# Attention and two feed-forward layers on one core: the last block's tokens staged in another tile ring, and three edits beside it

## The chip, the cores and the metric

The kernel runs on one core of one Trainium2 chip. The metric is the device time of one execution in microseconds (us); lower is better.

## The reference

```python
scores = scale * np.matmul(q, k.transpose(0, 1, 3, 2))       # 4 batches, 8 heads, 576 x 576, head size 64
scores = np.where(block_i >= block_j, scores, -1e9)           # blocks of 64 positions
attn   = softmax(scores);  x = attn @ v                       # -> 2304 tokens x 512
h = x @ w_in;   x = (h * sigmoid(h)) @ w_out                  # layer 1, 512 -> 2048 -> 512
h = x @ w_in2;  x = (max(h,0) + alpha * min(h,0)) @ w_out2    # layer 2, same sizes
```

All tensors are float32. The kernel keeps float32 accuracy by splitting each operand into a high part that TensorE can multiply and a low part that holds the rest; each product is then three matmuls (high x high, high x low, low x high; `three`, L1027).

## The kernel before, in words

**Tokens.** The 2304 tokens form nine blocks of 256 (T1, T2). Blocks 0 to 3 are positions 0 to 255 of the four batches, blocks 4 to 7 positions 256 to 511, and block 8 the last 64 positions of all four batches together.

**Stages.** Attention runs per batch and pair of heads as 32 jobs (L1017). Their outputs are the tokens of layer 1, kept in `x_all` in two places: blocks of even number in one, of odd number in the other (L517). Block 8 is written to DRAM instead (`x_last`, L992, 16 stores from all the late jobs) and read back by `load_last` (L525) as two tiles `xl` of 128x512 float32 once place 0 of `x_all` is free of block 6. Layer 1 runs in 72 steps `d` (L1380), mixed with the attention that feeds later blocks. Steps 0 to 15 are blocks 0 and 1, then each block has eight steps: block 6 has 48 to 55. Steps 56 to 58 are block 7 alone, 59 to 68 blocks 7 and 8 together, 69 to 71 block 8 alone. A step has three parts: `up1` (L1035, matmuls into PSUM tile `h`, two places), `act1` (L1068) and, one step later, `down1` (L1081). `store1` (L1103) turns a finished block with VectorE into tiles `x2e` and stores them to DRAM. Layer 2 then reads the blocks back (`load2`, L1127, tiles `xs`).

**`act1`** computes h * sigmoid(h): ScalarE writes tanh(h/2) to tile `t`, VectorE forms (t+1)*h in `t` (L1075), ScalarE copies the high part to `g`, and `split` (L329, low part at L335) computes the low part of `g` on GpSimd for blocks 2 to 6 and on VectorE for the others (L1077).

**Rings.** A tile tag has a fixed number of places, taken in the order of creation: tile number i waits until tile i minus the count is done with. Tag `t` (ff1 pool) has two, shared by the `t` tiles of `act1`, the `x2e` tiles of blocks up to 6, and the two `xl` tiles. Around step 56 the order of that ring is: `t` of step 56, two `x2e` of block 6, two `xl`, `t` of step 57, `t` of step 58. Tag `p` (att pool) has three places of the same 2 KB per partition, used for attention probabilities. The att pool is closed, and its memory reused by the pool ff2, when the first ff2 tile is made (L293).

**Weights of layer 2** are read twice. A first reading takes the largest absolute value (`scan_w`, L457: tiles `scani` in the two places of att tag `st`, `scano` in four of ff2 tag `scan`; the maximum at L469 on VectorE). `scale_w` (L489) turns it into a scale: `spread` (L444) carries a per-partition maximum to all partitions with one ScalarE copy into `ar` (the tag `ar2`), one 128-column matmul (L449) and one VectorE maximum (L451). `load2` for the first two blocks of layer 2 uses `spread` too (L1140). A second reading (`raw1i`, `raw1o`) splits the weights (L350, L386).

**Order.** Nothing is scheduled at run time: the kernel collects operations with an engine, a cost and a due time `at`, and `Plan.order` (L150) simulates the engines and writes out the order; of the operations ready at an engine's next free moment it takes the one with the lowest `at`. Each engine runs its own list strictly in order, waiting on semaphores. All DMAs but eight run through SyncE's list (SP), so a DMA whose data is late holds back those behind it. In the model a DMA costs 0.5 us of SP and `extra` of the shared queue (KiB / 350):

```python
dma_free = max(dma_free, start + min(o.cost, 0.63) + 0.65) + o.extra   # L200
o.end = dma_free + 0.95                                                # L201
```

Of the kernel before, what the change touches and what calls it, by code (L numbers as in the profile page):

```python
# [8 lines left out]
F32 = mybir.dt.float32  # L9
# [4 lines left out]
AF = mybir.ActivationFunctionType  # L14
# [15 lines left out]
T1 = 256  # L30
# [29 lines left out]
SLOTS = ((256, 256, 4), (384, 576, 10))  # L60

LEAD = 2.0
LOAD, PREPARE, PREPARE_V = -6.4, -2.5, -0.11
SCORES, WEIGHTS, NEXT, LAST, OUTPUT = 0.0, 0.4, 0.44, 1.03, 1.47

# [42 lines left out]
class Plan:  # L108
# [41 lines left out]
    def order(self):  # L150
        engines = {}
        for o in self.ops:
            engines.setdefault(o.engine, 0.0)
        ready = {e: [] for e in engines}
        blocked = {}
        heads = {tag: 0 for tag in self.rings}
        dma_free = 0.0

        def offer(o):

            new = {}
            for b in o.bufs:
                if not b.started:
                    old = b.order[b.index - b.bufs] if b.index >= b.bufs else None
                    if heads[b.tag] + new.get(b.tag, 0) != b.index or (old is not None and old.free_at is None):
                        blocked.setdefault(b.tag, []).append(o)
                        return
                    new[b.tag] = new.get(b.tag, 0) + 1
                    if old is not None:
                        o.ready = max(o.ready, old.free_at + 0.2)  # L170
            ready[o.engine].append(o)

        for o in self.ops:
            if not o.waits:
                offer(o)
        done = []
        while len(done) < len(self.ops):
            best = None
            for e, lst in ready.items():
                if not lst:  # L180
                    continue
                free = engines[e]
                start = max(free, min(o.ready for o in lst))
                if best is None or start < best[0]:
                    best = (start, e)
            assert best is not None, "the order of the tiles' places leaves nothing that can start"
            start, e = best
            o = min((o for o in ready[e] if o.ready <= start), key=lambda o: (o.at, o.index))

            fresh = [b for b in o.bufs if not b.started]  # L190
            lost = [b for b in fresh if b.index - heads[b.tag] != sum(c.tag == b.tag and c.index < b.index for c in fresh)]
            ready[e].remove(o)
            if lost:
                blocked.setdefault(lost[0].tag, []).append(o)
                continue
            o.start = start
            engines[e] = start + o.cost
            o.end = start + o.cost
            if e == "DMA":
                dma_free = max(dma_free, start + min(o.cost, 0.63) + 0.65) + o.extra  # L200
                o.end = dma_free + 0.95  # L201
            done.append(o)
            recheck = []
            for b in o.bufs:
                if not b.started:
                    b.started = True
                    heads[b.tag] += 1
                    recheck.append(b.tag)
                b.left -= 1
                if b.left == 0:  # L210
                    b.free_at = max(p.end for p, _, _ in b.accesses)
                    recheck.append(b.tag)
            for p in o.after:
                p.waits -= 1
                p.ready = max(p.ready, o.end + self.HOPS[e].get(p.engine, 0.0) + (p.slack if p.engine != e else 0.0))
                if not p.waits:
                    offer(p)
            for tag in recheck:
                for p in blocked.pop(tag, []):
                    offer(p)  # L220
        self.span = max(o.end for o in done)
        return sorted(done, key=lambda o: (o.start, o.index))
# [27 lines left out]
def block_causal_attention_silu_prelu(  # L250
# [16 lines left out]
    B, PAIRS = qkv_b.shape[:2]  # L267
    FIRST = 2
# [10 lines left out]
    plan = Plan()  # L279
# [8 lines left out]
    ff_p = ctx.enter_context(tc.tile_pool(name="ff1", bufs=1))  # L288
# [24 lines left out]
    def sb(pool, shape, dtype, tag, bufs=1, name=None):  # L313
        return Buf(plan, pool, shape, dtype, tag, bufs, name)
# [129 lines left out]
    def spread(src, reads, dst, writes, tag="o"):  # L444

        t = ps(tag)
        ar = sb(ff2_p, [128, 1], F32R, "ar2", 2)
        act(1, lambda: ar(), src, AF.Copy, reads, [ar])
        add("PE", 0.12, lambda: nc.tensor.matmul(  # L449
            t()[:, 0:128], ar().to_broadcast([128, 128]), eye_r(), start=True, stop=True), [ar, eye_r], [t])  # L450
        add("DVE", dve_cost(128), lambda: nc.vector.tensor_reduce(dst(), t()[:, 0:128], axis=AX.X, op=ALU.max), [t], writes)  # L451
# [73 lines left out]
    def load_last():  # L525
        x = x_parts(2 * B)
        for kk in range(0, KD, 2):
            t = sb(ff_p, [128, 2, T1], F32, "t", 2, name="xl")
            dma(lambda t=t: t(),
                lambda kk=kk: x_last()[kk * 128:(kk + 2) * 128].rearrange("(k p) t -> p k t", p=128), 256,  # L530
                [x_last], [t])
            split(2 * T1, lambda kk=kk: x()[:, 0, kk:kk + 2], lambda kk=kk: x()[:, 1, kk:kk + 2], lambda t=t: t(),
                  [t], [(x, (0, kk))], [(x, (1, kk))], "DVE")
# [534 lines left out]
    def act1(step):  # L1068

        h = hs.pop(step)  # L1070
        t = sb(ff_p, [128, 2, T1], F32, "t", 2)
        g = sb(ff_p, [128, 2, 2, T1], F32R, "g", 2)
        h3 = lambda: h().rearrange("p (c t) -> p c t", c=2)
        act(2 * T1, lambda: t(), h3, AF.Tanh, [h], [t], psum=True, scale=0.5)
        add("DVE", dve_cost(2 * T1), lambda: nc.vector.scalar_tensor_tensor(  # L1075
            t(), t(), 1.0, h3(), op0=ALU.add, op1=ALU.mult), [t, h], [t])
        split(2 * T1, lambda: g()[:, 0], lambda: g()[:, 1], lambda: t(), [t], [(g, 0)], [(g, 1)],  # L1077
              "POOL" if FIRST <= step[1][0] < 2 * B - 1 else "DVE")
        gs[step] = g

    def down1(step):  # L1081
# [298 lines left out]
    for d in range(-20, total + 1):  # L1380
        attend(d + 1.0)

        plan.at = float(d - AHEAD)
        for at in range(d + AHEAD):
            for w in need.get(at, []):
                if w in first:
                    first.remove(w)
                    load_w(0, *w)
        plan.at = d - 0.5
        for kind, m in need.get(d + 1, []):  # L1390
            split_w(0, kind, m, aside=d + 1 <= ASIDE and m % 2 == 1)
        if d < 0:
            continue
        plan.at = float(d)
        if d < total:
            up1(seq[d])
            plan.at = d + 0.3
            act1(seq[d])
        if d >= 1:
            plan.at = d + 0.5  # L1400
            down1(seq[d - 1])
            for n, m in sorted(set(seq[d - 1])):
                if m == edge[n][1]:
                    plan.at = d + 0.6
                    store1(n)
        if d == LAST_AT:
            assert not pieces
            load_last()

        if d == LAST_AT:  # L1410
            ends += [o for b in plan.rings["x_last"] for o, _, _ in b.accesses]
            for m in range(MF):
                plan.at = SCAN[2] + SCAN[3] * m
                scan_w("o", m, ends)
            scanned = scans[:]
        if d == SCAN_AT:
            for j, m in enumerate(order2[NOT_AHEAD:]):
                plan.at = SCAN[0] + SCAN[1] * j
                scan_w("i", m, ())
        if d == last_up[order2[0]] + 1:  # L1420
            for m in order2[:NOT_AHEAD]:
                plan.at = last_up[m] + 1.7
                load_w(1, "i", m)
                greatest("i", m, staged[1, "i", m])
            plan.at = last_up[order2[0]] + 1.0
            scale_w("i", ends)
            plan.at = SCAN[2] + SCAN[3] * MF
            scale_w("o", ends)
        for m in order2:
            if last_up[m] == d - 1:  # L1430
                plan.at = d + 0.7
                if m not in order2[:NOT_AHEAD]:
                    load_w(1, "i", m)
                split_w(1, "i", m)
        if d == (NB - 1) * ND + 2:
            load2(0, after=ends)
            plan.at += 2.0
            load2(1)
# [137 lines left out]
```

## Time and profile before

| | |
|---|---|
| three runs | 897.29, 898.02, 899.15 us (median 898.02) |
| the profiled execution | 898.74 us, of which the profiled span is 897.0 us and 1.7 us lie around it |
| busy share of the span | PE 98%, PE weight loads 84%, VectorE (DVE) 79%, ScalarE (ACT) 52%, GpSimd (POOL) 31% |
| DMA | 130 GB/s mean over the span |
| TensorE clock | 0.999 of full speed, 2.4 GHz |

In the profile's rows times are in us from the start of the span. A row of the timeline has start, duration, engine, line, operation, output <- inputs and, in square brackets, how long the engine sat idle before it and which event ended that wait. Neighbouring instructions of one kind are merged into one row (xN). PEld is the weight load of TensorE, which overlaps its matmuls (PE); SPq is SyncE issuing DMAs.

### The profile page before, as it was taken

To read this page: it belongs to the slowest core of one execution; us is meant where nothing else is said; L and a number is where in the kernel's file an instruction comes from. 1 tells how busy PE (TensorE), PEld (TensorE's weight loads), DVE (VectorE), ACT (ScalarE), POOL (GpSimd) and SP (SyncE) were. 2 spreads that over 40 slices of the span, in tenths; PEclk is the share of its full clock that TensorE was granted. 3 is DMA by queue.
4 is the path that set the end of the run, shared out by engine and by line. 5 is a ranking of instruction groups with operands and counts; after the bars stand their busy time and mean duration, and the time that the engine had idled before them with its cause. 6 is when DMAs were issued, how large, how long until landed. Compare 5 with 4: busy or idle time off the path is not lost.

```text
span 897.0 us, 18472 instructions
## 1 busy us (share of the span) xinstructions
PE 879.4 (98%) x6941; PEld 749.4 (84%) x6941; DVE 706.7 (79%) x1572; ACT 464.0 (52%) x1061; POOL 281.9 (31%) x412
## 2 busy tenths in 40 slices
PE   7899999999999999999999999999999999999997
PEld 5688888898898989888878887666888888888886
DVE  5999767688898888898458899898887867677574
ACT  6987556677777877776224774333322222222211
POOL 6601002232222312222100000357645445454552
PEclk9999999999999999999999999999999999999999
DMA  8962133567566675669788893242101110000010
GB/s 299 408 246 53 36 78 94 146 130 158 112 153 145 114 175 116 128 153 189 218 279 338 288 343 126 97 164 77 46 28 27 49 28 27 25 28 25 1 24 24
DMA packets 134249, 116.56 MB, mean 130 GB/s; under 512 B 100240, under 2 KB 111504, under 8 KB 134160
## 3 DMA queue, kind: packets, MB, share of 16 engines
q1 hardware_dynamic: 133008, 111.19, 44.8%
q0 software_dynamic: 1152, 4.19, 1.2%
q8 instruction: 54, 0.88, 0.5%
q14 instruction: 35, 0.29, 0.1%
HBM read 78.65 MB, written 14.16 MB: 103 GB/s over the span
## 4 chain that ended last, share of the span: by engine, by line
PE 62%; DMA 3%; DVE 2%; ACT 1%; issue 1%; POOL 0%; DVEq 0%; SPq 0%; ACTq 0%
PE h L1030 20%; PE acc L1030 18%; PE e L1030 12%; PE s L1030 5%; PE o L1030 3%; DMA scani<-w_in 2%; PE e L734 2%; PE o L908 1%; DMA raw1i<-w_in 1%; PE s L734 1%; PE o L918 0%; ACT p L325 0%; DVE stat L852 0%; DMA xl<-x_last 0%; DVE t L1075 0%
## 5 line engine op out<-in xcount | busy, mean ns | idle before, releaser
L1030 PE MATMUL h<-x_all,w0i 128*128 128x256 f32 (+1 forms) x1464 | 223.6, 304 | 2.2 <-DVE t L1075 1.3
L1030 PEld LDWEIGHTS h<-x_all,w0i 128*128 128x128 f32 x1464 | 200.2, 190 | 21.1 <-issue 3.8
L1030 PEld LDWEIGHTS <-w1i 128*128 128x128 f16 x1728 | 168.9, 98 | 23.3 <-issue 0.5
L1211 POOL TENSOR_TENSOR u<-u 128x128 f32<-128x128 f32 x224 | 136.0, 627 | 125.6 <-DVE u L1203 105.7
L325 ACT ACTIVATE g<-u 128x896 f16<-128x896 f32 (+1 forms) x72 | 63.2, 878 | 215.1 <-POOL u L1211 138.8
L1030 PE MATMUL acc<-w0o,g 128*128 128x512 f32 x672 | 168.5, 394 | 0.6 <-POOL g L335 0.6
L1030 PEld LDWEIGHTS <-g 128*128 128x128 f16 x1368 | 133.9, 98 | 32.7
L1030 PEld LDWEIGHTS acc<-w0o,g 128*128 128x128 f32 x672 | 122.5, 188 | 27.4 <-issue 2.5
L335 POOL TENSOR_TENSOR g<-t,g 128x512 fp32r<-128x512 f32 x40 | 53.0, 1326 | 162.2 <-ACT g L325 158.2
L1030 PE MATMUL acc<-xh,w1i 128*128 128x256 f16 x864 | 100.2, 273 | 0.0
L1030 PE MATMUL h<-xh,w1i 128*128 128x256 f16 x864 | 99.2, 273 | 0.0
L1224 DVE SCALAR_TENSOR_TENSOR g<-u,g 128x896 f16<-128x896 f32 (+1 forms) x72 | 76.4, 1062 | 10.6 <-ACT g L325 10.6
L325 ACT ACTIVATE p<-p,stat 128x512 f16<-128x512 f32 (+2 forms) x112 | 63.3, 608 | 23.0 <-ACT p4b L325 7.0
L1199 DVE TENSOR_SCALAR u<-acc,alpha_sb 128x256 f32<-128x256 f32 x72 | 32.2, 478 | 46.3 <-PE acc L1030 45.0
L325 ACT ACTIVATE p<-e,stat 128x256 f32<-128x256 f32 (+2 forms) x98 | 50.9, 526 | 33.4 <-DVE stat L946 22.3
L325 ACT ACTIVATE t<-h 128x512 f32<-128x512 f32 x72 | 42.9, 596 | 42.7 <-PE h L1030 37.1
L1030 PE MATMUL e<-w1om,g 128*128 128x256 f16 x504 | 64.2, 273 | 0.0
L1075 DVE SCALAR_TENSOR_TENSOR t<-t,h 128x512 f32<-128x512 f32 x72 | 49.0, 680 | 9.2 <-ACT t L325 8.1
L325 ACT ACTIVATE g<-t 128x512 fp32r<-128x512 f32 x72 | 45.3, 629 | 18.1 <-DVE t L1075 17.5
L885 DVE SCALAR_TENSOR_TENSOR p<-p,stat,p 128x384 f16<-128x384 f32 (+1 forms) x64 | 48.4, 796 | 4.3 <-ACT p L325 4.1
L1030 PE MATMUL e<-w1op,g 128*128 128x256 f16 (+1 forms) x264 | 49.5, 311 | 0.0
L1030 PE MATMUL e<-w0o,g 128*128 128x512 f32 x192 | 49.0, 393 | 0.0
(167 smaller groups left out, 1328.0 us busy)
## 6 DMA issues: line engine op xcount, KB each, us to landing
st<-qkv_b SPq DMA_DIRECT2D x16, 800.0 KB, 4.9
raw0i<-w_in SPq DMA_DIRECT2D x16, 512.0 KB, 9.9
raw0o<-w_out SPq DMA_DIRECT2D x16, 512.0 KB, 10.0
scano<-w_out SPq DMA_DIRECT2D x16, 512.0 KB, 6.5
raw1i<-w_in SPq DMA_DIRECT2D x16, 512.0 KB, 5.6
raw1o<-w_out SPq DMA_DIRECT2D x16, 512.0 KB, 5.2
scani<-w_in SPq DMA_DIRECT2D x13, 512.0 KB, 4.4
x<-x2e SPq DMA_DIRECT2D x18, 256.0 KB, 2.5
```

Of the source, the lines that this page charges most:

```text
L325: nc.scalar.activation(dst(), src(), func, **k)
L335: eng.tensor_tensor(lo(), src(), hi().bitcast(F32), op=ALU.subtract)
L734: yield lambda n=n, a=a, b=b: nc.tensor.matmul(dst, w[rows, a, q0:q0 + m], w[rows, b, nq + k0:nq + k1], start=(n == 0), stop=(n == 2))
L885: add("DVE", dve_cost(n, 1, 1), lambda hl=hl, rr=rr, pr=pr: nc.vector.scalar_tensor_tensor(hl()[:, :, 1], pr(), rr(), hl()[:, :, 0], op0=A ...
L908: nc.tensor.matmul(o()[64 * r:64 * r + 64, q0:T1], self.v(r, kt, cv), self.turned(r, kt, cp, q0), start=(kt == 0 and n == 0), stop=(kt == ...
L1030: nc.tensor.matmul(dst, lhs(a), rhs(b), start=(start and n == 0), stop=(stop and n == 2))
L1075: add("DVE", dve_cost(2 * T1), lambda: nc.vector.scalar_tensor_tensor(t(), t(), 1.0, h3(), op0=ALU.add, op1=ALU.mult), [t, h], [t])
L1199: add("DVE", dve2_cost(T2, 1), lambda c=c, m=m: nc.vector.tensor_scalar(u()[:, 2 * c:2 * c + 2].rearrange("p i t -> p (i t)"), h()[:, T2 * ...
L1211: add("POOL", pool2_cost(128, 2.5), lambda out_=out_, x=x, y=y, op=op: nc.gpsimd.tensor_tensor(u()[:, out_], u()[:, x], u()[:, y], op=op), ...
L1224: add("DVE", dve2_cost(blocks * 128, 0, True), lambda: nc.vector.scalar_tensor_tensor(side(1)(), src(), 2.0**-G_EXP, side(0)(), op0=ALU.mu ...
```

## The change

- `load_last` takes its two `xl` tiles from tag `p` of the att pool (three places) instead of tag `t`, its due time moves from d + 0.6 (that of block 6's stores) to d + 0.2, and the modelled size of each load from 256 to 700 KiB.
- In `act1` the low parts of block 6 are computed on VectorE instead of GpSimd.
- In `spread` the ScalarE copy counts in the model as done 1.5 us later, so the matmul after it is placed later in TensorE's list.
- In `Plan.order` a DMA is not started before the eighth last has landed.

```diff
+LATE = 1.5
+LANES = 8
@@ order
+        landed = []
...
                 free = engines[e]
+                if e == "DMA" and len(landed) >= LANES:
+                    free = max(free, landed[-LANES])
                 start = max(free, min(o.ready for o in lst))
...
             engines[e] = start + o.cost
-            o.end = start + o.cost
+            o.end = start + o.cost + (o.extra if e == "ACT" else 0.0)
             if e == "DMA":
                 dma_free = max(dma_free, start + min(o.cost, 0.63) + 0.65) + o.extra
                 o.end = dma_free + 0.95
+                landed.append(o.end)
@@ spread
-        act(1, lambda: ar(), src, AF.Copy, reads, [ar])
+        act(1, lambda: ar(), src, AF.Copy, reads, [ar]).extra = LATE
@@ load_last
-            t = sb(ff_p, [128, 2, T1], F32, "t", 2, name="xl")
+            t = sb(att_p, [128, 2, T1], F32, "p", 3, name="xl")
             dma(lambda t=t: t(),
-                lambda kk=kk: x_last()[kk * 128:(kk + 2) * 128].rearrange("(k p) t -> p k t", p=128), 256,
+                lambda kk=kk: x_last()[kk * 128:(kk + 2) * 128].rearrange("(k p) t -> p k t", p=128), 700,
@@ act1
-              "POOL" if FIRST <= step[1][0] < 2 * B - 1 else "DVE")
+              "POOL" if FIRST <= step[1][0] < 2 * B - 2 else "DVE")
@@ the main loop
         if d == LAST_AT:
             assert not pieces
+            plan.at = d + 0.2
             load_last()
```

## Rows read from the trace of the kernel before

**Rows 1.** The page, first part: busy time, share of the span, instructions.
```profile
PE 879.4 (98%) x6941; PEld 749.4 (84%) x6941; DVE 706.7 (79%) x1572; ACT 464.0 (52%) x1061; POOL 281.9 (31%) x412
```

**Rows 2.** Waits of PE from 380 to 545 us: total, times, longest.
```profile
PE h L1030 <- DVE t L1075: 1.3, 1, 1.3
PE o L449 <- ACT ar L325: 1.1, 1, 1.1
PE acc L1030 <- POOL g L335: 0.6, 1, 0.6
PE h L1030 <- DVE x_all L998: 0.2, 1, 0.2
```

**Rows 3.** Timeline from 446 to 455 us: block 6's stores, then `xl`.
```profile
446.24 1.91 SPq L317 DMA_DIRECT2D x<-x2e  x2
...
448.32 1.97 SPq L317 DMA_DIRECT2D xl<-x_last  x2
...
450.30 3.03 PE L1030 MATMUL h<-x_all,w0i 128*128 128x256 f32 x24
450.40 1.83 SPq L317 DMA_DIRECT2D scano<-w_out  x4
...
453.17 0.58 ACT L325 ACTIVATE t<-h 128x512 f32<-128x512 f32 x1
...
453.91 0.68 DVE L1075 SCALAR_TENSOR_TENSOR t<-t,h 128x512 f32<-128x512 f32 x1
...
454.64 2.35 PE L1030 MATMUL h<-x_all,w0i 128*128 128x512 f32 x9 [1.31 <-DVE t L1075]
```

**Rows 4.** Tile `x_last`, 420 to 460 us: two of its stores, both `xl` loads.
```profile
L317 SPq DMA_DIRECT2D x_last<-xf x2: 326/671/1016, 423.5 to 438.1; - x2
...
DMA to landing us min/median/max: 2.7/3.4/5.2
```

**Rows 5.** Timeline from 432 to 441 us: low part of step 54, block 7's tokens.
```profile
432.53 0.69 DVE L469 TENSOR_REDUCE wmaxi<-scani 128x1 f32<-128x512 f32 x1 [0.36 <-DMA scani<-w_in]
432.91 1.29 POOL L335 TENSOR_TENSOR g<-t,g 128x512 fp32r<-128x512 f32 x1 [9.80 <-ACT g L325]
...
434.25 0.50 PE L1030 MATMUL acc<-w0o,g 128*128 128x512 f32 x1 [0.55 <-POOL g L335]
...
439.62 0.48 DVE L998 SCALAR_TENSOR_TENSOR x_all<-o,sc,x_all 128x256 fp32r<-128x256 f32 x1
```

**Rows 6.** Chain that ended last, from 420 to 445 us.
```profile
434.55 4.45 DMA scani<-w_in
...
440.15 1.94 PE h L1030 x14
```

**Rows 7.** Timeline: L746 alone, and beside a low part on GpSimd.
```profile
377.99 0.87 DVE L746 SCALAR_TENSOR_TENSOR v<-st,sc,v 128x640 f16<-128x640 f32 x1
...
406.33 1.29 POOL L335 TENSOR_TENSOR g<-t,g 128x512 fp32r<-128x512 f32 x1
406.40 1.90 DVE L746 SCALAR_TENSOR_TENSOR v<-st,sc,v 128x640 f16<-128x640 f32 x1 [0.89 <-POOL v L743]
```

**Rows 8.** Windows of block 6: busy of PE, PEld, DVE, ACT, POOL; clock, DMA.
```profile
378.00:397.00 19.00, 19.00 (x173) 17.14 (x173) 16.68 (x43) 13.56 (x39) 3.59 (x4) 1.00 0.80 178
397.00:433.70 36.70, 36.70 (x319) 32.48 (x315) 28.02 (x73) 22.15 (x57) 6.92 (x7) 1.00 0.86 196
```

**Rows 9.** Timeline from 518 to 531 us: the product that waits, a later low part.
```profile
518.83 1.21 DVE L1136 TENSOR_REDUCE xsc<-xs 128x1 f32<-128x1024 f32 x1
...
520.43 0.33 PE L449 MATMUL o<-eye_r,ar 128*128 128x128 f32 x1 [1.07 <-ACT ar L325]
...
526.98 0.68 DVE L335 TENSOR_TENSOR g<-t,g 128x512 fp32r<-128x512 f32 x1
...
528.05 2.91 PE L1030 MATMUL acc<-w0o,g 128*128 128x512 f32 x12
```

**Rows 10.** Waits of SP from 0 to 60 us: total, times, longest.
```profile
SPq L317 <- DMA raw0i<-w_in: 11.5, 12, 1.4
```

## The prediction

> **What bounds the kernel now.** I read the page first. TensorE (PE) is busy for 879.4 of 897.0 us [rows 1], so a change pays only where it takes a gap out of PE's row or shortens PE's work; it does not touch PE's work. Next I asked PE's waits in the stretch the change reaches, 380 to 545 us. They are four single events, 1.31, 1.07, 0.55 and 0.21 us, 3.14 us together [rows 2]. Then the timeline around each: the 1.31 at 454.64 [rows 3], the 0.55 and 0.21 at 434.25 and 440.15 [rows 5, 6], the 1.07 at 520.43 [rows 9]. No more than 3.14 us, 0.35%, can be had there. The profiled execution took 898.74 us, 0.72 above the median of 898.02; the sum is made against 898.74, and the same gain is then taken from the median. The measurement can tell about 0.2%, 1.8 us, from no change.
>
> **The last block's tokens (`xl`).** PE waits 1.31 us at step 59 because its `h` place is free only after step 57's L1075, at 453.91 + 0.68 = 454.59. That instruction waits for tanh at 453.17, which waits for a place in ring `t`: the two `xl` tiles stand before it there, and they wait for block 6's `x2e` stores, so their loads go out only at 448.32 [rows 3]. Step 57's matmuls were over before those of step 58 began at 450.30, so tanh lost some 3 us.
> In ring `p` the load waits for the last `x_last` store only. That store goes out at 438.1; landings of this tile took 2.7 to 5.2 us [rows 4], so it is in DRAM by 443.3 at the latest. Two issues of some 0.4 us put SP at 444.1, ahead of the `x2e` stores due at 446.24, so the queue it is moved past is not held. With 2.7 us to land, the tokens are there by about 447, and their splits, each a ScalarE copy and a VectorE subtraction (0.68 us, as the low part in [rows 9]), end near 449. Step 57's tanh now needs the first `x2e` store landed: 446.24 + 2.7 = 448.9, then 0.58 and 0.68 give 450.2. PE asks for that place at 450.30 + 3.03 = 453.33, 3 us later. So the 1.31 us go; bounds 0 and 1.31, and I take 1.31 because of the 3 us to spare. What comes behind on SP is `scano`, at 450.40 now; its memory may lie over that of `p`, so it may have to wait for the splits near 449, which is still no later than now.
>
> **The product of a maximum.** Five products are made; only that of 520.43 holds PE, for 1.07 us: its input is copied after the maximum L1136, which ends at 518.83 + 1.21 = 520.04 [rows 9]. Put 1.5 us later in PE's list, it has about 12 matmuls of step 70 before it (3.03 / 24 = 0.126 us each [rows 3]), which need nothing from it. So PE arrives after 520.43. Its result is needed only by block 1's second-layer tokens, several us on. But PE is then 1.07 us earlier against VectorE, which the change does not speed up there. Next late is the low part that ends at 526.98 + 0.68 = 527.66; the third matmul of the group at 528.05 uses it, at 528.05 + 2 x 0.24 = 528.53, so 0.87 us are to spare [rows 9], and 0.20 of the 1.07 come back as a wait. I take 0.87; bounds 0 (if VectorE is late by more) and 1.07.
>
> **Block 6's low parts.** Eight leave GpSimd, 1.29 us each [rows 5], and come to VectorE at 0.68 us [rows 9]: 5.4 us more work there in about 60 us. For step 54 it decides a wait: GpSimd starts at 432.91 and PE waits until 434.25, 0.55 us. VectorE is in a scan maximum until 432.53 + 0.69 = 433.22, so the low part can end at 433.90 and PE waits some 0.25 instead [rows 5]. That 0.3 us does not reach the end: at 440.15 PE waits for L998, which stands in VectorE's list behind a scan maximum, and that waits for a DMA of 4.45 us begun at 434.55 [rows 5, 6]. PE arriving 0.3 earlier waits 0.3 longer. I take 0; bounds +0.76 (both waits gone, if the list puts L998 ahead of the maximum) and -0.68 (one low part put into the chain before L998).
> The other seven are hidden by PE's own work only while VectorE keeps up: it is busy 16.68 of 19.00 us before 397 and 28.02 of 36.70 after [rows 8]. Some of the load is given back: L746 takes 0.87 us alone and 1.90 us beside a low part on GpSimd [rows 7], 1.03 us that disappear with it. That makes D below less likely.
> The Trainium skill says why, in "SBUF — State Buffer", section "Who interferes with whom": a VectorE instruction with two SBUF inputs is fully blocked by a GpSimd instruction that reads SBUF and was issued first. The trace agrees: that L746 began 0.07 us after GpSimd's low part and ended 0.68 after it, about its own 0.87 alone. By the rule the same subtraction, itself one with two SBUF inputs, can now be blocked by GpSimd's other work, so the edit is no pure gain for VectorE; the sum is the same with it and without it, and without it D would have 0.12.
>
> **The DMA model.** SP already waited 12 times, 11.5 us in all, for earlier `raw0i` landings in the first 60 us [rows 10]; the model now knows it. That can put the first layer's weight loads in another order, and what is split when. From the trace of before I can only bound it by the longest such wait, 1.4 us either way; I take 0, the middle of the two, since nothing in the row says which side.
>
> **Sum.** 1.31 + 0.87 + 0 + 0 = 2.18 us: 898.74 becomes 896.56 with the profiler's execution, and 898.02 - 2.18 = 895.8 for the median, 0.24% faster.
>
> **Rivals.** (B) *All four waits go.* L998 stands ahead of the maximum in the new list and the product costs nothing back: 3.14 us, 894.9. For it: VectorE's list is written anew. Against it: the scan maximum still has a DMA to wait for and L998 is ready only shortly before. Chance 0.15.
> (C) *One of the two long waits stays in another form.* Either VectorE, in line with rows 9, gives back the whole product (gain 1.31, 896.7), or step 57's tanh is held by a late `x2e` store behind the early `scano` loads (gain 0.87, 897.2). For it: VectorE is the engine both chains run through; against it: 3 us to spare at the first. About 897.0, chance 0.22.
> (D) *VectorE becomes the bound in block 6*: the change is slower. Place: 378 to 434 us. It decides once the eight low parts no longer fit into VectorE's idle time in front of what PE waits for; before 397 that idle time is 19.00 - 16.68 = 2.3 us for some 2.4 steps, that is 1.6 us of new work, so 0.7 to spare. Price if nothing fits: 5.4 us, 898.02 - 2.18 + 5.4 = 901.2; half of it would give 898.5. For it: 88% busy; against it: PE shows no wait on VectorE in that stretch, and after 397 the idle time is nearly four times larger than before it. Chance 0.08.
> (E) *The new order does something else than intended*, new small waits in the first 60 us of up to 1.4 us or more: 898 to 899.5. Chance 0.05.
>
> **How the numbers follow.** The forecast has 0.50. Its own spread, from the bounds -0.68 and +0.76 of block 6 and 0.87 to 1.07 of the product, is 895.0 to 896.5; about 0.36 of its 0.50 lie beyond 1.8 us of gain. With B that is 0.51 for faster. C and the rest of the forecast make 0.36 for no change, D and E 0.13 for slower. The range from 894.6 to 898.9 takes in the forecast, B, C and half of E; D is left out.
>
> **What would show it.** Right: `xl` issued near 443 and ahead of `x2e`; step 59's matmuls following step 58's without a wait; the product after some 12 more matmuls with no wait; PE still waiting for L998 near 440. Wrong: a wait of PE on L1075 or on a low part after 520; waits of PE on low parts or probabilities between 380 and 434; a longer start. If PE's waits from 380 to 545 fall by 2 us and the time does not, the loss is outside that stretch, and my reading of what the change touches was too narrow.

## The result, and the profile after

The changed kernel takes 903.02 us (median of 10 executions) against 898.67 us of the kernel before (10 executions): a ratio of 1.0052, 95% interval 1.0034 to 1.0069. It is slower by half a per cent. The prediction was wrong: 895.8 us and its whole range lie below. The profiled execution took 902.50 us with a span of 900.7 us, 3.7 us more than the span before.

The page, first part, answers to [rows 1]; the waits of TensorE (PE) from 380 to 545 us answer to [rows 2]. The last fence has PE's longest waits of the whole span (total, times, longest).

```profile
PE 881.1 (98%) x6941; PEld 749.4 (83%) x6941; DVE 708.8 (79%) x1580; ACT 464.9 (52%) x1061; POOL 276.3 (31%) x404
```

```profile
PE h L1036 <- DVE x_all L1004: 2.8, 1, 2.8
```

```profile
PE e L596 <- DMA st<-qkv_first: 4.4, 1, 4.4
PE h L1036 <- DVE x_all L1004: 2.8, 1, 2.8
PE o L637 <- POOL p L630: 2.3, 1, 2.3
```

(Line numbers are 6 higher than before.) The first wait of 4.4 us was there before. The four waits of [rows 2] have become one: 1.31, 1.07 and 0.55 us are gone, and the fourth, on block 7's tokens, has grown from 0.21 to 2.79 us. A second new wait, 2.26 us, stands in the start, where I had looked at SyncE only. And PE's busy time rose by 1.7 us although its matmuls are the same 6941: some of them ran longer.

**The start.** Timeline of the changed kernel: GpSimd's last two scalings of the first jobs' probabilities, PE's wait for them, and a landmark, an instruction that waits for the same thing in both kernels.

```profile
42.09 6.96 POOL L630 TENSOR_SCALAR p<-p,stat 128x256 f32<-128x256 f32 x2 [0.69 <-DVE stat L621]
...
49.10 0.44 PE L637 MATMUL o<-eye_r,p 128*128 128x128 f32 x2 [2.26 <-POOL p L630]
...
150.52 0.95 PE L740 MATMUL e<-qk 64*128 64x128 f32 x11 [0.26 <-DVE x2e L1118]
```

The same instructions of the kernel before:

```profile
42.29 2.14 POOL L624 TENSOR_SCALAR p<-p,stat 128x256 f32<-128x256 f32 x2 [2.07 <-DVE stat L615]
...
146.81 0.95 PE L734 MATMUL e<-qk 64*128 64x128 f32 x11 [0.25 <-DVE x2e L1112]
```

Windows of the changed kernel around that wait (busy of PE, PEld, DVE, ACT, POOL; granted clock; DMA):

```profile
46.60:49.10 2.50, 0.25 (x3) 0.01 (x1) 2.10 (x4) 0.75 (x3) 2.45 (x1) 1.00 1.00 397
49.10:50.30 1.20, 1.20 (x6) 1.06 (x7) 0.00 (x0) 0.72 (x2) 0.00 (x0) 0.95 1.05 420
50.30:53.60 3.30, 3.30 (x13) 1.75 (x13) 1.89 (x4) 2.16 (x6) 0.00 (x0) 0.50 0.67 268
53.60:60.00 6.40, 6.40 (x30) 5.27 (x29) 6.02 (x12) 5.85 (x13) 0.00 (x0) 1.00 0.91 323
```

GpSimd needs 6.96 us for what took 2.14. PE stands 2.26 us, and about 1 us after it starts again its granted clock falls to 0.50, 1.2 GHz, for 3.3 us, which costs another 1.65 us (half of the 3.3 us in which PE is busy at half speed). The landmark is 3.7 us late, about the sum of the two (3.9).

**Block 7's tokens.** Timeline from 442 to 448 us; it answers to [rows 5, 6].

```profile
442.58 0.47 ACT L331 ACTIVATE x_all<-o,sc 128x256 fp32r<-128x256 f32 x1 [1.25 <-PE o L924]
...
444.02 0.69 DVE L475 TENSOR_REDUCE wmaxi<-scani 128x1 f32<-128x512 f32 x1 [1.97 <-DMA scani<-w_in]
...
446.19 0.69 DVE L475 TENSOR_REDUCE wmaxi<-scani 128x1 f32<-128x512 f32 x1 [1.48 <-DMA scani<-w_in]
446.79 0.48 DVE L1004 SCALAR_TENSOR_TENSOR x_all<-o,sc,x_all 128x256 fp32r<-128x256 f32 x1
...
447.32 1.94 PE L1036 MATMUL h<-x_all,w0i 128*128 128x256 f32 x14 [2.79 <-DVE x_all L1004]
```

L1004 (L998 before) could start when ScalarE's copy ends, 443.05. VectorE's list has two scan maxima ahead of it, each waiting for its load, so it starts 3.7 us later. In the kernel before two maxima stood between the same two instructions, and the delay was 2.6 us:

```profile
436.51 0.47 ACT L325 ACTIVATE x_all<-o,sc 128x256 fp32r<-128x256 f32 x1 [0.73 <-PE o L918]
...
439.02 0.69 DVE L469 TENSOR_REDUCE wmaxi<-scani 128x1 f32<-128x512 f32 x1 [1.39 <-DMA scani<-w_in]
```

So most of the lateness is not made here: ScalarE's copy itself comes 6.1 us later than before, 3.7 of it from the start and the rest from the last attention job, which experiment 2 follows.

Where the 3.7 us of span come from, by these rows: +3.7 at the start; 2.79 in place of 0.55 + 0.21, +2.0; -1.31 and -1.07 for the two waits that went. That makes 3.4 of 3.7.

### The profile page after: what moved, and what is told of

Read it like the earlier page. It is cut to its first block, busy times and chain, and to the rows that moved or that the text cites. A ratio compares the mean times of both kernels' runs of the same rounds, so it can differ in the third digit from the quotient of the medians.

```text
span 900.7 us, 18466 instructions
## 1 busy us (share of the span) xinstructions
PE 881.1 (98%) x6941; PEld 749.4 (83%) x6941; DVE 708.8 (79%) x1580; ACT 464.9 (52%) x1061; POOL 276.3 (31%) x404
## 4 chain that ended last, share of the span: by engine, by line
PE 63%; DMA 4%; DVE 1%; ACT 1%; issue 0%; DVEq 0%; SPq 0%; ACTq 0%
PE h L1036 20%; PE acc L1036 18%; PE e L1036 13%; PE s L1036 5%; DMA scani<-w_in 3%; PE o L1036 3%; PE e L740 2%; PE o L914 1%; DMA raw1o<-w_out 1%; PE s L740 1%; PE o L924 0%; DVE wmaxi L475 0%; DVE osb L1322 0%; ACT p L331 0%; DVE stat L858 0%
## 5 line engine op out<-in xcount | busy, mean ns | idle before, releaser
L1036 PE MATMUL acc<-w0o,g 128*128 128x512 f32 x672 | 170.6, 396 | 0.1
L341 POOL TENSOR_TENSOR g<-t,g 128x512 fp32r<-128x512 f32 x32 | 42.6, 1332 | 123.4 <-ACT g L331 119.4
L1081 DVE SCALAR_TENSOR_TENSOR t<-t,h 128x512 f32<-128x512 f32 x72 | 49.1, 682 | 17.0 <-ACT t L331 15.6
L422 POOL DMA_DIRECT2D kept<-wso x8 | 4.8, 602 | 166.4 <-DMA raw1i<-w_in 96.0
```

The source lines that it names most:

```text
L341: eng.tensor_tensor(lo(), src(), hi().bitcast(F32), op=ALU.subtract)
L422: add("POOL", 1.5, lambda: nc.gpsimd.dma_start(kept[s](), both().rearrange("p c n -> p (c n)")), [a, b], [kept[s]])
L1036: nc.tensor.matmul(dst, lhs(a), rhs(b), start=(start and n == 0), stop=(stop and n == 2))
```

## The experiments

The expectations name theories by letters. S: the DMA limit rewrites the start, GpSimd's scalings are stretched, PE stands and its clock falls (S2: the contest with VectorE does it). V: block 6's low parts load VectorE, the last job comes late, and with it block 7's tokens. K: a long wait of PE costs more than itself through its clock. G: PE, earlier by the `xl` edit, meets late loads. R1 and R2 are rivals of S and V.

Each line has the median, the ratio to the kernel before with its interval, the profiled span and the mean granted clock over the timed executions. Beside kernels 1 to 15 the kernel before had medians of 897.8 to 898.4 us and a mean clock of 0.9986 to 0.9992. At 900 us, 0.001 of clock is 0.9 us.

| kernel | us | ratio | span | mean clock |
|---|---|---|---|---|
| changed (first time) | 903.02 | 1.0052 [1.0034, 1.0069] | 900.7 | 0.9969 |
| 1 before + DMA limit | 898.90 | 1.0011 [0.9997, 1.0025] | 899.7 | 0.9989 |
| 2 before + block 6 on VectorE | 900.87 | 1.0030 [1.0018, 1.0042] | 897.7 | 0.9977 |
| 3 before + `xl` + later product | 899.64 | 1.0013 [1.0001, 1.0024] | 899.6 | 0.9990 |
| 4 changed - DMA limit | 903.07 | 1.0053 [1.0035, 1.0070] | 899.2 | 0.9964 |
| 5 before + later product | 897.61 | 0.9989 [0.9976, 1.0002] | 894.8 | 0.9990 |
| 6 before + `xl` | 899.11 | 1.0001 [0.9986, 1.0016] | 899.5 | 0.9987 |
| 7 before + three long waits | 919.47 | 1.0227 [1.0204, 1.0250] | 917.7 | 0.9905 |
| 8 later product, low parts moved too widely | 906.62 | 1.0091 [1.0071, 1.0111] | 904.3 | 0.9980 |
| 9 changed, again | 901.98 | 1.0036 [1.0019, 1.0053] | 900.9 | 0.9973 |
| 10 changed - block 6 | 899.22 | 1.0018 [1.0005, 1.0032] | 897.4 | 0.9987 |
| 11 later product + step 54 | 896.83 | 0.9987 [0.9976, 0.9998] | 894.8 | 0.9993 |
| 12 before + first four steps of block 6 | 898.65 | 1.0004 [0.9991, 1.0017] | 897.1 | 0.9986 |
| 13 changed, third time | 902.37 | 1.0055 [1.0036, 1.0073] | 900.8 | 0.9977 |
| 14 changed - DMA limit, again | 899.85 | 1.0024 [1.0007, 1.0041] | 898.0 | 0.9978 |
| 15 changed, two scalings on VectorE | 901.38 | 1.0043 [1.0028, 1.0057] | 898.6 | 0.9977 |

Kernels 1 to 4, 5 to 8, 9 to 12 and 13 to 15 each ran together on one chip.

### 1. The DMA limit alone

```diff
+                if e == "DMA" and len(landed) >= LANES:
+                    free = max(free, landed[-LANES])
```

> The kernel before with the DMA limit alone. Theory S (the limit rewrites the order of the first-layer weight loads and splits, GpSimd's scaling of the last first-job probabilities is held up by VectorE, TensorE stands and its clock then falls): about 4 us slower than before, a wait of TensorE of 1.5 to 3 us on GpSimd's p near 49 us, and a granted clock under 0.7 somewhere between 50 and 55 us. Rival R1 (the stretched GpSimd scaling is an accident of that execution and not tied to the limit): within 1 us of before, no such wait. Rival R2 (the limit also delays the late scan loads and so block 7's tokens): in addition a wait of over 2 us on the attention output copy x_all near 440 us, 6 us or more slower in all.

Measured: 0.5 us above before in the median, which the interval doesn't part from zero, and no wait on `p` over 0.4 us. Up to 370 us its planned order is the changed kernel's, yet GpSimd's pair took another time here:

```profile
42.67 4.75 POOL L630 TENSOR_SCALAR p<-p,stat 128x256 f32<-128x256 f32 x2 [0.69 <-DVE stat L621]
```

4.75 us instead of 2.14 or 6.96: stretched, but early enough for PE. S doesn't hold as written; R1 has the time right and not the reason, since the stretch is there. The limit alone is not enough for the wait on `p`. The x_all wait of R2 isn't there. (The profiled execution, 901.51 us, is among its higher ones: the product's wait is 2.49 us in it, and the clock 0.50 from 522.5 to 525.8 us.)

### 2. Block 6's low parts on VectorE alone

```diff
-              "POOL" if FIRST <= step[1][0] < 2 * B - 1 else "DVE")
+              "POOL" if FIRST <= step[1][0] < 2 * B - 2 else "DVE")
```

> The kernel before with block 6's low parts on VectorE alone. Theory V (the moved low parts push the last job's probabilities back in VectorE's list by about 3 us, and two more scan maxima then stand ahead of block 7's tokens): TensorE waits 2.5 to 3 us on x_all near 440 to 447, the 0.55 us wait is gone, about 2 us slower than before. Rival R2 (that wait comes from the DMA limit): the wait stays at 0.2 us and the time is 0.3 to 0.6 us better.

Measured: V. The timeline of this kernel shows the chain:

```profile
433.34 0.75 DVE L985 SCALAR_TENSOR_TENSOR p<-p,stat,p 128x512 f16<-128x512 f32 x1 [0.18 <-ACT p L331]
...
440.29 0.69 DVE L475 TENSOR_REDUCE wmaxi<-scani 128x1 f32<-128x512 f32 x1 [1.92 <-DMA scani<-w_in]
...
442.26 0.69 DVE L475 TENSOR_REDUCE wmaxi<-scani 128x1 f32<-128x512 f32 x1 [1.28 <-DMA scani<-w_in]
442.86 0.47 DVE L1004 SCALAR_TENSOR_TENSOR x_all<-o,sc,x_all 128x256 fp32r<-128x256 f32 x1
...
443.39 1.94 PE L1036 MATMUL h<-x_all,w0i 128*128 128x256 f32 x14 [2.57 <-DVE x_all L1004]
```

The last job's probabilities in the kernel before:

```profile
430.62 0.75 DVE L979 SCALAR_TENSOR_TENSOR p<-p,stat,p 128x512 f16<-128x512 f32 x1 [0.84 <-ACT p L325]
```

They come 2.7 us later here. L1004 then falls behind later scan maxima and ends at 443.33 instead of 440.10 [rows 5], 3.2 us later.

Most of the 2.7 us arise between 408 and 417 us: against the kernel before, an earlier job's probabilities are 0.8 us early near 408 and the next one's 1.6 us late near 415. There VectorE isn't busier than before but idler, although two of the moved low parts (0.68 us each) stand there: two scan maxima wait 2.2 us for their loads, and the second of them has moved ahead of a job's probabilities. This kernel, then its window:

```profile
411.20 0.69 DVE L475 TENSOR_REDUCE wmaxi<-scani 128x1 f32<-128x512 f32 x1 [1.30 <-DMA scani<-w_in]
...
414.07 0.69 DVE L475 TENSOR_REDUCE wmaxi<-scani 128x1 f32<-128x512 f32 x1 [0.89 <-DMA scani<-w_in]
```

```profile
408.00:417.00 9.00, 9.00 (x61) 7.68 (x61) 6.59 (x19) 3.65 (x11) 0.00 (x0) 1.00 1.08 253
```

The kernel before, the same maxima and the same window:

```profile
410.87 0.68 DVE L469 TENSOR_REDUCE wmaxi<-scani 128x1 f32<-128x512 f32 x1
...
416.65 0.62 DVE L469 TENSOR_REDUCE wmaxi<-scani 128x1 f32<-128x512 f32 x1
```

```profile
408.00:417.00 9.00, 9.00 (x61) 7.77 (x60) 7.83 (x22) 4.76 (x15) 1.29 (x1) 1.00 0.95 245
```

Counted in the traces, 9 maxima of `scani` stand ahead of the last job's probabilities and 13 ahead of L1004 in each of the seven kernels with all of block 6 on VectorE (2, 4, 14, 15 and the three runs of the changed one). It is 8 and 12 in kernel 12, and 7 and 11 in the kernel before and in the eight others. So the edit changes what the planner puts ahead of the last job, and the delay goes with that count. How much of it the low parts would make in an unchanged list wasn't tried.

The span grows by 0.7 us (2.57 for 0.76, and 1.31 gone, are 0.5 of it; one `xl` load is between the stores now). The median grows by 2.5: the mean clock is lower by 0.0012, 1.1 us, and the profiled execution, 899.49 us, is the lowest of the 12.

### 3. The two other edits together

> The kernel before with the two edits xl in ring p and the later product, without the DMA limit and with block 6 on GpSimd. If the two waits go as the prediction said: 2.2 us faster than before (1.31 and 0.87), no wait of TensorE on VectorE's t near 454, none on ar near 520, the waits of 0.55 and 0.21 us near 434 and 440 unchanged. Rival (their gain comes back as later waits): less than 1 us faster.

Measured: the rival, and worse: 1.2 us slower than before. The edits are those of kernels 5 and 6; what PE meets is shown under 6.

### 4 and 14. The changed kernel without the DMA limit

```diff
-LANES = 8
+LANES = 1000000
```

> The changed kernel without the DMA limit. Theories S and V together: the start as before, the wait on x_all of 2.5 to 3 us stays, the waits of 1.31, 1.07 and 0.55 us are gone: 0.2 to 0.5 us faster than before, no difference that can be measured, and some 4 us faster than the changed kernel. Rival R2 (the limit causes both losses): 2.5 to 2.9 us faster than before, x_all wait at most 0.3 us.

> The changed kernel without the DMA limit once more. If the start's loss of 3.8 us is in most executions of the changed kernel: 2 to 4 us faster than the kernel of the run before this one, the two scalings in 2.1 us. Rival (it is in few of them, or is made up for elsewhere): within 1 us of it, as in the first comparison, with falls of the clock or waits of TensorE behind x_all that the first profile of this kernel did not have.

Measured: the start is that of before (GpSimd's pair in 2.1 us), the x_all wait stays, at 2.31 and 3.56 us. Both times the clock fell in it or behind it. Windows of kernel 14:

```profile
440.00:443.70 3.70, 0.14 (x3) 0.01 (x1) 1.14 (x3) 0.00 (x0) 0.00 (x0) 1.00 0.37 127
...
444.60:447.90 3.30, 3.30 (x14) 2.91 (x13) 0.69 (x1) 0.73 (x2) 0.00 (x0) 0.50 0.31 115
```

R2 is out: the limit doesn't make the x_all wait. But the time of kernel 4 misses what was expected: no faster than the changed kernel, and 0.5% slower than before where no difference was expected. What the limit costs in the median isn't settled: nothing by kernel 4, 2.5 us by 14 beside 13. The executions of 4 lost 1.3 us more to the clock than those of 14 (0.9964 and 0.9978) with the same code.

### 5. The later product alone

```diff
-        act(1, lambda: ar(), src, AF.Copy, reads, [ar])
+        act(1, lambda: ar(), src, AF.Copy, reads, [ar]).extra = LATE
```

> The kernel before with the later product alone. As predicted: the 1.07 us wait on ar near 520 is gone, the waits of 1.31, 0.55 and 0.21 us stand, 0.87 to 1.07 us faster in the span. Rival (VectorE gives it back): a wait on a low part g near 528, less than 0.3 us faster.

Measured: as predicted. The waits of this kernel from 380 to 545 us:

```profile
PE h L1036 <- DVE t L1081: 1.2, 1, 1.2
PE h L1036 <- DVE x_all L1004: 0.3, 1, 0.3
```

No wait on `ar`, none on `g`: VectorE gives nothing back. 0.75 us faster in the median, which the interval doesn't part from zero. The 0.55 us wait is missing too, with no edit to it.

### 6. The `xl` tiles alone

```diff
-            t = sb(ff_p, [128, 2, T1], F32, "t", 2, name="xl")
+            t = sb(att_p, [128, 2, T1], F32, "p", 3, name="xl")
```

(with the later size, 700 KiB, and the earlier due time)

> The kernel before with the xl tiles in ring p alone. As predicted: the 1.31 us wait near 454 is gone and nothing takes its place, 1.3 us faster. Rival G (from the run with both edits: TensorE, earlier by 1.3 us, meets VectorE standing in its list behind maxima of scano and xs that wait for their loads): new waits of TensorE on g between 455 and 470 us of 1.5 us or more together, 0.2 to 1 us slower than before, more where the clock falls after them.

Measured: G in its kind. The 1.31 us wait is gone, and new ones come 6 us later:

```profile
460.09 0.17 DVE L486 TENSOR_REDUCE amax<-alpha_sb 128x1 f32<-128x16 f32 x1 [0.69 <-DMA alpha_sb<-alpha]
...
460.92 2.57 PE L1036 MATMUL e<-w0o,g 128*128 128x512 f32 x10 [0.73 <-DVE g L341]
...
462.69 1.22 DVE L1142 TENSOR_REDUCE xsc<-xs 128x1 f32<-128x1024 f32 x1 [1.83 <-DMA xs<-x]
...
464.62 0.69 DVE L475 TENSOR_REDUCE wmaxo<-scano 128x1 f32<-128x512 f32 x1 [0.70 <-DMA scano<-w_out]
465.22 0.68 DVE L1081 SCALAR_TENSOR_TENSOR t<-t,h 128x512 f32<-128x512 f32 x1
...
466.62 1.90 PE L1036 MATMUL acc<-w0o,g 128*128 128x512 f32 x6 [0.41 <-ACT g L331]
```

The low part that PE waits for at 460.92 stands in VectorE's list behind the maximum of `alpha`, and L1081, whose result PE needs next, behind maxima of `xs` and `scano`; each of these waits for its load. The new waits are 1.14 us together, less than the 1.5 that G asked for, against 1.31 gone. No gain shows in the median (the interval is 1.4 us either way). In kernel 3 the same place shows 1.38 + 0.44 us, and the clock at 0.50 from 468.6 to 471.9 us; in kernel 10, 1.48 us. In the changed kernel it shows none; there PE is late by then, through the start and block 7's wait.

### 7. What a long wait costs

```diff
+        if step[0] in ((2, 8), (3, 8), (4, 8)):
+            plan.ops[-1].cost = 0.01
+            for _ in range(6):
+                add("POOL", 0.01, lambda: nc.gpsimd.tensor_tensor(
+                    g()[:, 1], t(), g()[:, 0].bitcast(F32), op=ALU.subtract), [t, (g, 0)], [(g, 1)])
```

> The kernel before in which GpSimd computes the low part of one step of blocks 2, 3 and 4 seven times over (same values), which the order does not know of: three waits of TensorE of some 2 to 4 us each, in stretches that have no wait before. Theory K (a wait of this length costs more than itself, since TensorE's granted clock falls to half for some us after part of such waits): the span grows by the three waits and by 1.5 to 2 us for each fall that the windows show, and the mean clock over the executions is 0.995 to 0.998 against 0.999. Rival (the clock has nothing to do with the waits): the time grows by the waits alone and the mean clock stays at 0.999.

Measured: K. Waits of PE from 100 to 545 us, then windows at the three places:

```profile
PE acc L1036 <- POOL g L1088: 14.4, 3, 6.1
```

```profile
176.90:183.60 6.70, 5.67 (x22) 3.92 (x22) 1.88 (x3) 1.10 (x2) 3.23 (x4) 0.50 0.34 117
...
245.10:251.90 6.80, 5.38 (x15) 4.46 (x16) 4.48 (x9) 2.57 (x10) 3.59 (x4) 0.50 0.54 115
316.80:320.10 3.30, 3.30 (x8) 2.62 (x9) 2.18 (x2) 0.00 (x0) 2.23 (x3) 0.50 0.45 84
```

Each fall begins in the wait or right at its end, and PE then works at 1.2 GHz: 5.67 + 5.38 + 3.30 = 14.35 us at half speed, 7.2 us lost. 14.4 + 7.2 - 1.07 (the product's wait, absent here) is 20.5; the span grew by 20.7. A wait of 4 to 6 us cost half as much again. The mean clock was lower than I expected.

### 8. A miss

```diff
+              "POOL" if FIRST <= step[1][0] < 2 * B - 2 or (step[1][1] // 2 != 6) else "DVE")
```

> The kernel before with the later product, and of block 6's low parts that of step 54 alone on VectorE. The waits of 1.07 and 0.55 us go, the wait on x_all near 440 grows from 0.21 to at most 0.8 us, since the last job is not delayed: 0.9 to 1.2 us faster than before. Rival (one low part is enough to delay the last job): a wait on x_all of over 1.5 us and no gain.

The condition as written holds for every block, so the low parts of blocks 0, 1, 7 and 8 went to GpSimd too, but for one step each. It tells nothing on step 54; kernel 11 does. What it shows is the start: from 30 to 100 us nine low parts on GpSimd took 1576 ns each (11 on VectorE took 697 before), and PE waits there.

```profile
L341 POOL TENSOR_TENSOR g<-t,g 128x512 fp32r<-128x512 f32 x9 | 14.2, 1576 | 28.2 <-ACT g L331 28.2
```

### 9, 13 and 10. The changed kernel again, and without block 6's edit

> The changed kernel once more, beside the next one on the same chip. Theory V with K: the wait on x_all of 2.3 to 2.8 us near 443 to 447 is there again, while the start comes without the 2.26 us wait on GpSimd's p (an accident of the first profile); mean granted clock over the executions 0.996 to 0.998, 0.4 to 0.6% slower than before. Rival S (the start belongs to the change): the wait on p of over 1.5 us and a low clock near 50 us again.

> The changed kernel a third time, on the same chip as the next two. Theory S2 (the DMA limit's order stretches GpSimd's last two scalings; whether TensorE has to stand for them is decided by which of the two engines gets the second one through): the two scalings take 4.7 or 7.0 us together, against 2.1 without the limit. Mean granted clock 0.996 to 0.998, 0.3 to 0.5% slower than before.

> The changed kernel with block 6's low parts on GpSimd again. Theory V with K (block 6 on VectorE is what costs): no wait on x_all over 0.5 us, mean clock back to 0.999, 3 to 4 us faster than the changed kernel, at most 0.1% from before. Rival S (the DMA limit and its start cost): within 1 us of the changed kernel.

Measured: 9 and 13 repeat the first profile: GpSimd's pair in 7.0 us, a wait of 2.2 us at 49.3, the clock at 0.50 behind it, the x_all wait (2.25 and 2.55 us). So S is right that the start is no accident of one execution, against my expectation for 9. Kernel 10 has block 6 undone and is 2.8 us faster than 9 beside it, with the clock back near that of before; its x_all wait is 0.88 us, more than the 0.5 I allowed, and it stays 0.0018 above before, like kernel 3. But this pair doesn't price V. In kernel 10's profile GpSimd's pair takes 4.75 us and PE doesn't wait for it, so its landmark is at 147.26 against 150.60 in 9: 3.3 us, nearly all of the 3.5 by which the two spans differ. What the smaller x_all wait gains, the wait of 1.48 us on `g` near 466 takes back. That the start's wait goes when an edit near 400 us is undone has no explanation here. The price of block 6 by itself is kernel 2's.

### 11. Later product and step 54 alone

```diff
+              "POOL" if FIRST <= step[1][0] < 2 * B - 2
+              or step[1][0] == 2 * B - 2 and (step[1][1] // 2 != 6) else "DVE")
```

> The kernel before with the later product and the low part of step 54, and of no other step or block, on VectorE. The waits of 1.07 and 0.55 us go, that on x_all near 440 is 0.2 to 0.8 us: 1.0 to 1.4 us faster than before (0.9988 to 0.9984), and the start as before. Rival (this one low part also pushes the last job back): a wait on x_all of over 1.5 us, no faster than before.

Measured: 1.2 us faster than before, the one kernel here whose whole interval lies below 1. Its waits from 380 to 545 us are 1.2 us on `t` and 0.2 us on x_all. Kernel 5, without step 54, has the same span, so the gain is the product's; that step 54 adds to it isn't shown.

### 12. Half the load

```diff
+              "POOL" if FIRST <= step[1][0] < 2 * B - 2
+              or step[1][0] == 2 * B - 2 and (step[1][1] // 2 >= 4) else "DVE")
```

> The kernel before with the low parts of block 6's first four steps alone on VectorE. Theory V as a matter of load (each low part on VectorE pushes the last job's probabilities back a little): the last job's L1004 ends some 1 us later than before, and TensorE waits on x_all for 0.8 to 1.6 us, about half of what all eight cost. Rival (only low parts near the last job matter): a wait of at most 0.4 us.

Measured: an x_all wait of 1.52 us, with L1004 ending at 441.57, 1.5 us later than before. Four low parts, done long before the last job's output, make about half the delay that eight make (1.5 of 3.2 us), so they need not be near the last job. That it is VectorE's load isn't shown: from 408 to 417 us, where the delay arises, VectorE is busy for less than in the kernel before (6.23 us against 7.83), and waits 1.26 and 1.47 us for scan loads.

```profile
408.00:417.00 9.00, 9.00 (x60) 7.58 (x59) 6.23 (x17) 4.06 (x12) 1.29 (x1) 1.00 1.05 207
```

### 15. The two scalings off GpSimd

```diff
-                add("POOL", pool_cost(n), lambda r=r: nc.gpsimd.tensor_scalar(
+                late = (self.b, self.pair) == (FIRST - 1, PAIRS - 1) and i == 1
+                eng2 = nc.vector if late else nc.gpsimd
+                add("DVE" if late else "POOL", dve_cost(n) if late else pool_cost(n),
+                    lambda r=r, eng2=eng2: eng2.tensor_scalar(
```

> The changed kernel with the last two scalings of the first jobs' probabilities on VectorE in place of GpSimd, the DMA limit kept. Theory S2: no wait of TensorE on p of over 0.5 us after 45 us, no low clock near 50 us, offset to the kernel before at 60 us at most 0.7 us; the wait on x_all near 443 of 2.3 to 2.8 us stays; 1 to 3 us faster than the changed kernel. Rival (the start's loss has another cause, such as SyncE's blocked weight loads): a wait of over 1.5 us on another tile before 60 us and no gain.

Measured: S2. With the DMA limit kept there is no new wait before 60 us, the clock stands, and the landmark is at 147.26 instead of 150.5 to 150.8:

```profile
48.00:56.00 8.00, 8.00 (x41) 6.42 (x41) 8.00 (x16) 7.74 (x19) 0.00 (x0) 1.00 1.03 409
```

The scalings take 0.34 us each on VectorE. SyncE's loads aren't the cause. That it is VectorE which stretches the scalings on GpSimd is read from the rows beside them, not tried. 1.0 us faster than 13 in the median, too little for six executions of each to tell, and 3.5 at the landmark; in the profile the x_all wait, 2.82 us, has a fall of the clock behind it that kernel 13 doesn't have.

## Why the prediction was wrong

**The DMA model** was taken at 0 with bounds of 1.4 us from SyncE's longest wait [rows 10]. That is the step that fails first in the span. The cost comes in on another engine: GpSimd's pair is stretched, PE stands 2.2 us, and the clock falls. The landmark is 3.7 to 3.9 us late in three profiles of three. I had bounded a change of order by a wait on the queue that is reordered, and not by what stands on the engines behind it; no row of GpSimd's scalings was read. Two things stay open. How the limit stretches the pair isn't shown: the VectorE instructions beside the first scaling come in the same order as before. And with the limit but block 6 on GpSimd (kernels 1 and 10) PE doesn't wait; there the landmark is only 0.5 us late, and the medians are 0.5 and 1.2 us above before.

**Block 6's low parts** were taken at 0, at worst -0.68. The step "PE arriving 0.3 earlier waits 0.3 longer" looked at one low part next to L998. The other seven I took as hidden while VectorE keeps up, and priced their failure (rival D) by waits of PE inside block 6. VectorE did keep PE fed there, but the last job, which nobody waits for until 440 us, came late. The step that failed is that VectorE's idle time, 8.7 us after 397, was counted as room. The engine works its list in order, and 3.15 us of that time in the kernel before are one wait for a scan load, a little ahead of the last job's probabilities:

```profile
428.53 0.69 DVE L469 TENSOR_REDUCE wmaxi<-scani 128x1 f32<-128x512 f32 x1 [3.15 <-DMA scani<-w_in]
```

The list written with the edit has two more scan maxima ahead of that job. In the changed kernel's rows this costs 2.0 us, and kernel 2, which has this edit alone, is 2.5 us above before. This is the best-shown part of the loss. D had the right engine and the wrong place; it had 0.08.

**The `xl` tiles**: the wait went as worked out, and `xl` was issued at 443.66 with the stores behind it. That this is near the forecast 443 is luck: the last `x_last` store had moved to 443.28 from 438.1. The term of 1.31 us failed all the same. In kernels 3, 6 and 10 waits of 1.1 us and more come up behind it, and no gain is left: I checked what PE meets at step 57, not what it meets 6 to 12 us later. In the changed kernel the gain stays, as I read it because PE is late there anyway; that wasn't tried by itself.

**The product**: the mechanism was right. 0.87 was taken; the wait is gone in every kernel that has the edit, and in kernels 5 and 11 none came back on `g` near 528. The medians gave 0.75 and 1.2 us.

**What no step had**: the price of a wait. Each of the terms was a wait in us. Rows of before show no fall of the clock, so I took 2.4 GHz as given. With all of block 6 on VectorE the mean clock over the executions is 0.9964 to 0.9978 in seven series, without it 0.9986 to 0.9993 (kernel 7 apart, and kernel 8). As an estimate from these clocks that is 1 to 2 us on top of the waits themselves.

The prediction's test for too narrow a reading was waits from 380 to 545 us that fall by 2 us without the time. They fell by 0.35, from 3.14 to 2.79; the rest of the loss lay outside, in the start, which I had left to one row.

## What to carry to other kernels

When an order is planned as a whole, a change of its model moves work everywhere: bound it by the engines whose work is moved, and ask for each shared helper (here GpSimd's scalings) how late it may be, not only for the queue that the model speaks of. The idle time of an engine that works a list in order is not room for more work when it is spent waiting for a load: ask what the engine waits for, and what the new list puts ahead of the late things, up to the place where somebody waits for them. A new wait of TensorE is to be priced with the fall of its clock that may follow, here 1.65 us for each 3.3 us at half speed, and a wait taken away is a gain only if what PE meets next is early as well.

## What the runs showed of the hardware

**GpSimd beside VectorE.** One 128x256 scaling on GpSimd (the first of the pair) took 0.73 us before and 3.83 us in each of the five profiles that have the DMA limit and the pair on GpSimd, with the same VectorE instructions beside it in the same order. VectorE's rows of the changed kernel:

```profile
42.47 0.68 DVE L377 SCALAR_TENSOR_TENSOR ws0o<-raw0o,ws0o 128x512 int32<-128x512 int32 x1
43.07 0.68 DVE L385 SCALAR_TENSOR_TENSOR w0i<-ws0i,w0i 128x512 fp32r<-128x512 f32 x1
43.67 0.68 DVE L341 TENSOR_TENSOR g<-t,g 128x512 fp32r<-128x512 f32 x1
```

The same three of the kernel before:

```profile
42.68 0.88 DVE L371 SCALAR_TENSOR_TENSOR ws0o<-raw0o,ws0o 128x512 int32<-128x512 int32 x1
43.48 0.68 DVE L379 SCALAR_TENSOR_TENSOR w0i<-ws0i,w0i 128x512 fp32r<-128x512 f32 x1
44.08 0.88 DVE L335 TENSOR_TENSOR g<-t,g 128x512 fp32r<-128x512 f32 x1
```

Either VectorE is held twice for 0.2 us, or GpSimd for over 3 us. The Trainium skill, "SBUF — State Buffer", section "Who interferes with whom", says that of two such instructions the one issued first has the shared ports and the other is blocked until it ends. Here the trace differs: GpSimd's instruction began at 42.09 by the profile, 0.38 us ahead of the first of these, and didn't end before 45.9, when five such instructions of VectorE had begun after it and ended; PE's wait until 49.10 bears out the late end. When it began, a VectorE instruction with one input was running in both kernels, so that doesn't tell them apart. What decides between the two outcomes isn't settled; VectorE and ScalarE run the same instructions in the same order up to 365 us in kernels 1 and 10 as in the changed kernel, and there GpSimd's second scaling took 0.94 us, where it took 3.16 in the changed kernel each time.

**The clock.** In ten profiles PE stands 2.2 us or more at once behind another engine; in eight of them the granted clock was 0.50 for 3.3 us or more during one such wait or right behind it (not in kernel 2, and in kernel 8 at another place). Not each such wait is followed by it: the x_all wait of the changed kernel was not in any of its three profiles, that of kernels 4, 14 and 15 was in all three. Shorter waits had it too: 1.38 + 0.44 us in kernel 3, 0.70 + 0.81 in kernel 6 (clock 0.50 from 44.9 to 48.2 us), 1.17 in kernel 8. The pair of kernel 6 stands in the kernel before as well, 0.68 + 0.81 us, with no fall. I had read the steady 1.00 of before as a property of the kernel, and it is one of what PE happens to meet.
